# An attention and MLP kernel ordered by a list scheduler: one batch's attention cut in two, and new durations in the scheduler's table

## The chip, the cores and the metric

The kernel runs on one core of one Trainium2 chip. The metric is the device time in microseconds (us) of one execution. TensorE does the matrix products (PE; its weight loads are PEld), VectorE is DVE, ScalarE ACT, GpSimd POOL, and SyncE (SP) issues all DMAs, in order.

## The reference

Three parts run one after the other. `q`, `k`, `v` have 4 batches, 8 heads, 576 rows and 64 columns; the two MLPs see 2304 rows of width 512.

```
scores = scale * q @ k.T                        # 576 x 576 for each of 32 heads
kth    = the 32nd largest score of a row
attn   = softmax(scores where scores >= kth)
x      = (attn @ v), heads side by side         # 2304 x 512

h = x @ w_in;  x = (h * cos(h)) @ w_out         # first MLP: 512 -> 2048 -> 512

P = exp(x @ w_gate - max); 8 rounds of row and column normalisation over all 2304 rows
out = sum over 8 experts e of P[:, e] * (max(x @ w1[e], 0) @ w2[e])   # 512 -> 1024 -> 512 each
```

The column sums of `P` need the logits of all rows, so the weighted sum over experts can't be finished before the last row has left the first MLP. The products of the experts themselves need no `P`.

## The kernel before, in words

Rows are counted in tiles of 128, 18 in all. The stages, in program order:

1. Decoding: `w_in` and `w_out` come as 64-bit floats and are turned to 32 bits on DVE, ACT and POOL (`decode`, 32 blocks).
2. The first three tiles of batch 0 (`LEAD`): attention and first MLP in plain fp32 (`attention_tile`, `moe1_tile_a`, `moe1_tile_b`; L629, L638 and L654 are their matrix products).
3. `attention(0, 3)`: the other rows of batch 0. Here and below each fp32 number is split in a high and a low part, and a product is three passes (L372 to L374; L383, L384, L387).
4. `fill(e, 0, 3)` for 8 experts: the first three tiles through every expert, unweighted, kept in DRAM (`y_d`) until `P` is known. These products read `x2fh` and `x2fl`.
5. `attention(1)`, then the first MLP for rows 384 to 895 (`moe1(Part(384))`: "the second block"). Its input is read back from DRAM (`x_d`) by `load_cols` into `xh` and `xl`, 4 pieces of 128 columns; piece d holds the head pair d.
6. `attention(2)`, `attention(3)`, and `fill(e, 3, 4)` for 8 experts: the second block through the experts.
7. The other three blocks of the first MLP, the normalisation, and the experts for the other 11 tiles.

In `attention` a head pair at a time is prepared (`prep_head`: keys, queries and values are loaded and split, on ACT and POOL). A row tile then goes through `att_tile`: scores on PE (L447, L448), copied by ACT; the 32nd largest is found on DVE by MAX8 (L459, L465) and MATCH_REPLACE (L464) in turn; the mask and row sum are one DVE instruction (L466); PE transposes the weights (L475), ACT and DVE split them (L493, L494). `att_out` multiplies with the values (L501 and L503, 9 matrix products for a head and group of rows), and the result is stored to `x_d`. Rows 0 to 255 and rows 256 to 575 of a head are such groups. A tile is 128 rows of one head, or the last 64 rows of two heads.

The order on each engine is fixed at build time. Every operation is put on a list with an estimated duration, and `Plan.issue` plays the list through: whichever engine is free first takes, of the operations whose inputs are ready by the estimates, the one with the lowest number in `PRIORITY` (L29), then the earliest in the program. On PE the order is first attention, first MLP, later attention, later MLP; on DVE the MLPs come ahead of later attention. The estimates are only used for the order: at run time each engine takes its instructions one by one and waits where an input is late.

An operation's inputs are known by buffer and interval. `load_cols` depends on the stores to `x_d` that overlap its rows: rows 384 to 895 are batch 0's rows 384 to 575 and batch 1's rows 0 to 319, so that in the kernel before it waits for both row groups of a head of batch 1, the second of which ends at row 575. Its input piece d is waited for on its own, since the products of the four pieces are separate operations (L701 to L710).

Of the kernel before, what the change touches and what calls it, by code (L numbers as in the profile page):

```python
# [12 lines left out]
I32 = mybir.dt.int32  # L13
# [57 lines left out]
class Plan:  # L71
# [78 lines left out]
    def issue(self):  # L150
        ops = self.ops
        for op in ops:
            op.outs, op.left, op.ready = [], len(op.deps), 0.0
        for k, op in enumerate(ops):
            for d in op.deps:
                ops[d].outs.append(k)
        engines = ("PE", "ACT", "DVE", "POOL", "SP")
        soon = {e: [] for e in engines}
        now = {e: [] for e in engines}
        free = dict.fromkeys(engines, 0.0)  # L160
        dma_free, func, warm, window, busy = 0.0, None, False, -1, {}
        for k, op in enumerate(ops):
            if not op.left:
                heapq.heappush(soon[op.eng], (0.0, k))
        order = []
        while len(order) < len(ops):
            best = None
            for e in engines:
                if now[e]:
                    t = free[e]  # L170
                elif soon[e]:
                    t = max(free[e], soon[e][0][0])
                else:
                    continue
                if best is None or t < best[0]:
                    best = (t, e)
            t, e = best
            while soon[e] and soon[e][0][0] <= t:
                k = heapq.heappop(soon[e])[1]
                heapq.heappush(now[e], (ops[k].prio, k))  # L180
            k = heapq.heappop(now[e])[1]
            op = ops[k]
            cost = op.cost
            if op.func and op.func != func:
                cost, func = cost + 1283.0, op.func
            if e == "PE":
                w = int(t / 3413)
                if w != window:
                    past = busy.get(w - 1, 0.0) / 3413
                    warm = past > 0.95 or (warm and past > 0.5)  # L190
                    window = w
                cost *= 1.0 if warm else 2.0
                a = t
                while a < t + cost:
                    z = min(t + cost, (int(a / 3413) + 1) * 3413.0)
                    busy[int(a / 3413)] = busy.get(int(a / 3413), 0.0) + z - a
                    a = z
            free[e] = op.end = t + cost
            if e == "SP":
                dma_free = max(t + cost + 650.0, dma_free) + op.bytes / 360.0  # L200
                op.end = dma_free + 900.0
            order.append(k)
            for o in op.outs:
                n = ops[o]
                n.ready = max(n.ready, op.end + self.LAT.get((e, n.eng), 130.0))
                n.left -= 1
                if not n.left:
                    heapq.heappush(soon[n.eng], (n.ready, o))
        self.estimate = max(op.end for op in ops)
        for k in order:  # L210
            ops[k].emit()


def mm_ns(n):
    return max(107.0, n / 2.4 + 3.0)


def act_ns(n, psum=False, ap=False):
# [11 lines left out]
def fused_kernel(tc, kq, vv, w_in, w_out, w_gate, w1, w2, out, B=4):  # L230
# [84 lines left out]
    def decode(src, keep, part):  # L315

        raw, mag, sgn, low = d_raw(), d_mag(), d_sgn(), d_low()  # L320
        dma(lambda: raw.ap, lambda: src.bitcast(I32), 1 << 19, writes=[raw])
        hi = lambda dt: raw.ap.bitcast(dt).rearrange("p (n t) -> p n t", t=2)[:, :, 1]
        lo = lambda: raw.ap.bitcast(U32).rearrange("p (n t) -> p n t", t=2)[:, :, 0]
        magf = lambda: mag.ap.bitcast(F32)
        put("DVE", 335, lambda: V.tensor_scalar(mag.ap, hi(I32), 3, 0x40000000, op0=ALU.logical_shift_left, op1=ALU.bitwise_xor), [raw], [mag])
        put("ACT", 613, lambda: A_.activation(sgn.ap, hi(F32), AF.Identity, bias=cols.ap[:, 1:2]), [raw, cols], [sgn])
        put("ACT", 613, lambda: A_.activation(sgn.ap, sgn.ap, AF.Sign, bias=cols.ap[:, 2:3]), [sgn, cols], [sgn])
        put("ACT", 520, lambda: A_.activation(low.ap, lo(), AF.Copy, scale=2.0**-52), [raw], [low])
        put("ACT", 520, lambda: A_.activation(magf(), magf(), AF.Abs), [mag], [mag])
        put("POOL", 1225, lambda: G_.tensor_tensor(magf(), magf(), sgn.ap, op=ALU.mult), [mag, sgn], [mag])  # L330
        put("DVE", 335, lambda: V.tensor_scalar(sgn.ap.bitcast(I32), mag.ap, -8388608, None, op0=ALU.bitwise_and), [mag], [sgn])
        put("POOL", 1225, lambda: G_.tensor_tensor(low.ap, low.ap, sgn.ap, op=ALU.mult), [low, sgn], [low])
        put("POOL", 1225, lambda: G_.tensor_tensor(low.ap, magf(), low.ap, op=ALU.add), [mag, low], [low])
        dma(keep, lambda: low.ap, 1 << 18, [low], [part])
# [84 lines left out]
    rr_r = ring_of("m1", 3, [128, 1024], F32, "rr")  # L419
    tt_r = ring_of("m1", 1, [128, 1024], F32, "tt")  # L420

    def prep_head(b, h):
        bh = b * H + h
        raw, kh, kl, qs, qt, vraw, vs = (r() for r in (kq_r, kh_r, kl_r, qs_r, qt_r, vraw_r, vs_r))
        dma(lambda: raw.ap, lambda: kq[bh], 1024 * S, writes=[raw])
        split_cols((kh, lambda: kh.ap), (kl, lambda: kl.ap), (raw, lambda: raw.ap[:, 0, :]), S)
        for o, lo, c0, n in ((qs, 0, 0, 512), (qt, 64, 512, 64)):
            v = lambda r, o=o, lo=lo, n=n: o.ap[r, lo : lo + n]
            w = lambda r, c0=c0, n=n: raw.ap[r, 1, c0 : c0 + n]
            put("ACT", act_ns(n), lambda v=v, w=w: A_.activation(v(slice(0, 128)), w(slice(0, 128)), AF.Copy), [raw], [o])  # L430
            put("POOL", pool_ns(n), lambda v=v, w=w: G_.tensor_tensor(v(slice(64, 128)), w(slice(64, 128)), v(slice(64, 128)).bitcast(F32), op=ALU.subtract), [raw, o], [o])
        dma(lambda: vraw.ap, lambda: vv[bh], 128 * 1280, writes=[vraw])
        split_cols(((vs, 0, 1), lambda: vs.ap[:, :, 0:64]), ((vs, 1, 2), lambda: vs.ap[:, :, 64:128]), (vraw, lambda: vraw.ap), 5 * D)
        return dict(kh=kh, kl=kl, qs=qs, qt=qt, vs=vs)

    def att_tile(stats, dests, plain=None):
# [24 lines left out]
        put("ACT", act_ns(S, ap=True), lambda: A_.activation(ex.ap, sc.ap, AF.Exp, scale=0.125, bias=mc(32)), [sc, (m, 32, 33)], [ex], func="exp")  # L461
        for r in range(3):
            src = wk if r else sc
            put("DVE", 669, lambda r=r, src=src: V.match_replace(wk.ap, mc(8 * r, 8), src.ap, LOWEST), [src, (m, 8 * r, 8 * r + 8)], [wk])  # L464
            put("DVE", 669, lambda r=r: V.max(mc(8 * r + 8, 8), wk.ap), [wk], [(m, 8 * r + 8, 8 * r + 16)])  # L465
        put("DVE", 729, lambda: V.scalar_tensor_tensor(ex.ap, sc.ap, mc(31), ex.ap, op0=ALU.is_ge, op1=ALU.mult, accum_out=mc(33)),  # L466
            [sc, ex, (m, 24, 32)], [ex, (m, 33, 34)])
        put("POOL", 162, lambda: G_.tensor_scalar(mc(34), mc(33), 1e-9, 1.0, op0=ALU.add, op1=ALU.mult), [(m, 33, 34)], [(m, 34, 35)])
        put("DVE", 75, lambda: V.reciprocal(mc(35), mc(34)), [(m, 34, 35)], [(m, 35, 36)])  # L469
# [65 lines left out]
        work = "mlp"  # L535
        return x_f

    def attention(b, done=0):

        nonlocal work  # L540
        work = "attention"
        for pr in range(4):
            hds = [prep_head(b, 2 * pr + j) for j in range(2)]

            def begin(hd):
                hd["ath"], hd["atl"] = ath_r(), atl_r()

            def end(j, s0, n, pr=pr, hds=hds):
                x32 = x32_r()
                att_out(hds[j], x32, j, n)  # L550
                t0 = b * S + s0
                r = slice(64 * j, 64 * j + 64)
                dma(lambda: x_d.ap[r, pr, t0 : t0 + n], lambda: x32.ap[r, :n], 256 * n, [x32],
                    [(x_d, (2 * pr + j) * NT + t0, (2 * pr + j) * NT + t0 + n)], slow=True)

            for t0 in (0, 2):
                tiles = range(max(t0, done), t0 + 2)
                for j, hd in enumerate(hds):
                    if tiles or t0:
                        begin(hd)  # L560
                    for t in tiles:
                        att_tile([(hd["qs"], t * 128, hd)], [(0, 128, hd, (t - tiles[0]) * 128)])
                    if tiles and not t0:
                        end(j, tiles[0] * 128, 128 * len(tiles))
            n = 128 * len(tiles)
            att_tile([(hds[0]["qt"], 64, hds[0]), (hds[1]["qt"], 0, hds[1])], [(0, 64, hds[0], n), (64, 64, hds[1], n)])
            for j in range(2):
                end(j, 512 - n, 64 + n)
        work = "mlp"


# [433 lines left out]
    n0 = LEAD * 128  # L1005
    for e in range(NE):
        fill(e, 0, LEAD, two)
    attention(1)
    eng_g = "DVE"
    moe1(Part(n0, two, keep_parts(x2fh, x2fl)), 3)  # L1010
    eng_g = "POOL"
    for b in range(2, B):
        attention(b)
    for e in range(NE):
# [79 lines left out]
```

## Time and profile before

| | |
|---|---|
| median of 3 runs | 2482.4 us (2480.79 to 2483.55) |
| profiled execution | 2480.47 us |
| its span, first to last instruction | 2478.7 us |
| PE, DVE busy in the span | 2364.7 us, 1986.9 us |
| ACT, POOL busy in the span | 1271.7 us, 1266.6 us |

The profile is of one execution. Its page gives busy times and the span in 40 slices; the trace behind it can be asked for the busy time of each engine in any stretch, for what an engine waited for, and for single instructions in order of time. A matrix product on PE is drawn longer than it occupies the array: in a run of them the next one starts before the last has ended, so the distance between two starts is what one costs, and gaps of less than about 0.2 us don't show as idle time.

### The profile page before, as it was taken

How to read it: one execution, taken by the hardware profiler on the slowest of the kernel's cores; microseconds unless marked ns; L12 is line 12 of the kernel's file. 1: busy time of each engine (PE TensorE's matmuls, PEld its weight loads, DVE VectorE, ACT ScalarE, POOL GpSimd, SP SyncE). 2: the span in 40 equal slices, each digit the busy share in tenths (PEclk: the TensorE clock that was granted, in tenths of full speed). 3: DMA queues.
4: the chain of work that ended last, by engine and by line, in shares of the span. 5: the costliest groups of instructions: out<-in, count | busy, mean ns of one | idle time of the engine just before them, and what ended most of it. 6: DMA issues, size and time to landing. Idle time of an engine off the chain costs nothing.

```text
span 2478.7 us, 33516 instructions
## 1 busy us (share of the span) xinstructions
PE 2364.7 (95%) x11089; PEld 1905.7 (77%) x11089; DVE 1986.9 (80%) x3651; ACT 1271.7 (51%) x2438; POOL 1266.6 (51%) x1328
## 2 busy tenths in 40 slices
PE   6878999999889999999999999999999999999999
PEld 3434688888667877778878888788888888888887
DVE  8997599999998999999986787776666666666655
ACT  6785566666578666666566776322322222322221
POOL 6886487767577656656520033433443334443330
PEclk9889999999899999999999999999999999999999
DMA  8765654444323333333334333022222221111101
GB/s 263 232 210 186 200 167 144 139 123 151 109 74 97 114 115 115 115 119 97 97 114 123 91 108 104 27 64 81 81 85 81 73 60 35 36 42 43 35 22 47
DMA packets 159501, 261.37 MB, mean 105 GB/s; under 512 B 15008, under 2 KB 60656, under 8 KB 159328
## 3 DMA queue, kind: packets, MB, share of 16 engines
q1 hardware_dynamic: 159328, 259.24, 34.5%
q8 instruction: 87, 1.43, 0.2%
q14 instruction: 86, 0.70, 0.1%
HBM read 227.31 MB, written 31.87 MB: 105 GB/s over the span
## 4 chain that ended last, share of the span: by engine, by line
PE 57%; DVE 28%; POOL 6%; issue 4%; ACT 3%; DMA 1%; SPq 0%; POOLq 0%; ACTq 0%; DVEq 0%
PE y L372 9%; PE y L373 9%; PE y L374 9%; DVE wk L464 7%; DVE m L465 6%; DVE ex L466 4%; PE g L374 2%; PE g L373 2%; PE g L372 2%; DVE m L459 2%; POOL wlo L347 2%; DVE atl L494 1%; PE y L383 1%; PE y L387 1%; PE y L384 1%
## 5 line engine op out<-in xcount | busy, mean ns | idle before, releaser
L347 POOL TENSOR_TENSOR wlo<-raw,whi 128x512 fp32r<-128x512 f32 x336 | 451.7, 1349 | 195.1 <-ACT whi L345 116.3
L465 DVE MAX8 m<-wk 128x8 f32<-128x576 f32 x432 | 318.1, 748 | 1.9
L953 DVE SCALAR_TENSOR_TENSOR acc<-y,P,acc 128x512 f32<-128x512 f32 x308 | 229.2, 748 | 103.5 <-PE y L374 103.2
L345 ACT ACTIVATE whi<-raw 128x512 fp32r<-128x512 f32 x416 | 259.2, 627 | 96.5 <-PE y L374 36.9
L464 DVE MATCH_REPLACE8 wk<-m,wk 128x576 f32<-128x576 f32 x288 | 213.5, 742 | 1.1
L372 PE MATMUL y<-whi,gh 128*128 128x512 f32 x448 | 182.0, 406 | 0.0
L372 PE MATMUL y<-gh,xh 128*128 128x512 f32 x450 | 177.1, 393 | 1.0 <-DVE acc L949 1.0
L374 PE MATMUL y<-whi,gl 128*128 128x512 f32 x448 | 176.5, 394 | 0.0
L373 PE MATMUL y<-gl,xh 128*128 128x512 f32 x450 | 176.5, 392 | 0.0
L374 PE MATMUL y<-gh,xl 128*128 128x512 f32 x450 | 176.2, 392 | 0.0
L373 PE MATMUL y<-wlo,gh 128*128 128x512 f32 x448 | 176.0, 393 | 0.0
L475 PE MATMUL t<-ident,ex 128*128 128x128 f32 (+1 forms) x720 | 136.6, 290 | 39.7 <-POOL ex L470 10.9
L457 ACT ACTIVATE sc<-s 128x288 f32<-128x288 f32 x288 | 117.0, 406 | 95.6 <-DVE ex L466 54.9
L475 PEld LDWEIGHTS t<-ident,ex 128*128 128x128 f32 (+1 forms) x720 | 85.9, 140 | 101.6 <-POOL ex L470 27.8
L466 DVE SCALAR_TENSOR_TENSOR ex<-sc,m,ex 128x576 f32<-128x576 f32 x144 | 152.8, 1061 | 3.6 <-ACT ex L461 1.8
L470 POOL TENSOR_SCALAR ex<-ex,m 128x576 f32<-128x576 f32 x144 | 111.2, 772 | 33.9 <-DVE m L469 33.0
L493 ACT ACTIVATE ath<-t 64x128 fp32r<-64x128 f32 (+3 forms) x272 | 104.5, 396 | 46.2 <-PE t L475 40.0
L461 ACT ACTIVATE ex<-sc,m 128x576 f32<-128x576 f32 x144 | 111.3, 773 | 32.4 <-POOL m L460 31.4
L459 DVE MAX8 m<-sc 128x8 f32<-128x576 f32 x144 | 106.9, 743 | 9.2 <-ACT sc L457 9.1
L464 DVE MATCH_REPLACE8 wk<-m,sc 128x576 f32<-128x576 f32 x144 | 106.7, 741 | 0.0
L372 PEld LDWEIGHTS y<-gh,xh 128*128 128x128 f32 x450 | 85.2, 189 | 20.0 <-DVE acc L949 1.8
L372 PE MATMUL y<-gh,gh 128*128 128x512 f32 x254 | 99.4, 391 | 0.0
(376 smaller groups left out, 7054.6 us busy)
## 6 DMA issues: line engine op xcount, KB each, us to landing
raw<-in_w_dram SPq DMA_DIRECT2D x384, 256.0 KB, 2.6
kq<-in_kq_dram SPq DMA_DIRECT2D x32, 576.0 KB, 4.3
raw<-win_d SPq DMA_DIRECT2D x64, 256.0 KB, 3.0
raw<-wout_d SPq DMA_DIRECT2D x64, 256.0 KB, 2.7
y_d<-st SPq DMA_DIRECT2D x56, 256.0 KB, 3.0
raw<-y_d SPq DMA_DIRECT2D x56, 256.0 KB, 2.7
wp<-win_d SPq DMA_DIRECT2D x24, 512.0 KB, 5.3
wp<-wout_d SPq DMA_DIRECT2D x24, 512.0 KB, 4.4
```

The costliest lines, as they stand in the source:

```text
L345: put("ACT", act_ns(n), lambda: A_.activation(hv(), rv(), AF.Copy), [rb], [hb])
L347: put(e, c, lambda: f.tensor_tensor(lv(), rv(), hv().bitcast(F32), op=ALU.subtract), [rb, hb], [lb])
L372: T_.matmul(o(), ah(), bh(), start=start, stop=False)
L373: T_.matmul(o(), ah(), bl(), start=False, stop=False)
L374: T_.matmul(o(), al(), bh(), start=False, stop=stop)
L457: put("ACT", act_ns(288, psum=True), lambda c=c: A_.activation(sc.ap[:, c], o(), AF.Copy), [ps_s], [(sc, c.start, c.stop)])
L459: put("DVE", 669, lambda: V.max(mc(0, 8), sc.ap), [sc], [(m, 0, 8)])
L464: put("DVE", 669, lambda r=r, src=src: V.match_replace(wk.ap, mc(8 * r, 8), src.ap, LOWEST), [src, (m, 8 * r, 8 * r + 8)], [wk])
L465: put("DVE", 669, lambda r=r: V.max(mc(8 * r + 8, 8), wk.ap), [wk], [(m, 8 * r + 8, 8 * r + 16)])
L466: put("DVE", 729, lambda: V.scalar_tensor_tensor(ex.ap, sc.ap, mc(31), ex.ap, op0=ALU.is_ge, op1=ALU.mult, accum_out=mc(33)), [sc, ex, (m, ...
L475: T_.transpose(pt()[:p, c - c0, :], ex.ap[:, c * 128 : c * 128 + p], ident.ap)
L953: put("DVE", 663, lambda y=y, av=av, pcol=pcol: V.scalar_tensor_tensor(av(), y.ap, pcol(), av(), op0=ALU.mult, op1=ALU.add), [y, P, a], [a])
```

## The change

`attention(b, done, stop)` now takes an end as well as a start, in tiles. Batch 1 is done as `attention(1, 0, 3)`, rows 0 to 383 of each head, and `attention(1, 3)`, rows 384 to 575. Between the two calls stands the second block's first MLP, which needs rows 0 to 319 of that batch. Heads are prepared anew by each call: keys and values whole, queries only those that the call uses (also in `attention(0, 3)`). The row groups of a head of batch 1 were 256 and 320; they are 256, 128 and 192.

The durations that `Plan.issue` works with are changed in five places: the decoding's two DVE operations (335 to 600 ns, twice), a matrix product (n/2.4 + 3 to n/2.4 + 13.6 ns for n columns), MATCH_REPLACE (669 to 738), the mask with its row sum (729 to 960), and the DMA rate (360 to 280 bytes per ns). They change no instruction, only the order.

```diff
-                dma_free = max(t + cost + 650.0, dma_free) + op.bytes / 360.0
+                dma_free = max(t + cost + 650.0, dma_free) + op.bytes / 280.0
...
-    return max(107.0, n / 2.4 + 3.0)
+    return max(107.0, n / 2.4 + 13.6)
...
-    def prep_head(b, h):
+    def prep_head(b, h, q0, q1):
...
-        for o, lo, c0, n in ((qs, 0, 0, 512), (qt, 64, 512, 64)):
+        for o, lo, c0, n in [(qs, q0, q0, min(q1, 512) - q0)] + [(qt, 64, 512, 64)] * (q1 > 512):
...
-    def attention(b, done=0):
+    def attention(b, done=0, stop=5):
...
-            hds = [prep_head(b, 2 * pr + j) for j in range(2)]
+            hds = [prep_head(b, 2 * pr + j, done * 128, min(stop * 128, S)) for j in range(2)]
...
-                tiles = range(max(t0, done), t0 + 2)
+                tiles = range(max(t0, done), min(t0 + 2, stop))
+                last = t0 and stop == 5
...
-                    if tiles or t0:
+                    if tiles or last:
...
-                    if tiles and not t0:
+                    if tiles and not last:
                         end(j, tiles[0] * 128, 128 * len(tiles))
-            n = 128 * len(tiles)
-            att_tile([(hds[0]["qt"], 64, hds[0]), (hds[1]["qt"], 0, hds[1])], [(0, 64, hds[0], n), (64, 64, hds[1], n)])
-            for j in range(2):
-                end(j, 512 - n, 64 + n)
+            if stop == 5:
+                n = 128 * len(tiles)
+                att_tile([(hds[0]["qt"], 64, hds[0]), (hds[1]["qt"], 0, hds[1])], [(0, 64, hds[0], n), (64, 64, hds[1], n)])
+                for j in range(2):
+                    end(j, 512 - n, 64 + n)
...
-    attention(1)
+    attention(1, 0, 3)
     eng_g = "DVE"
     moe1(Part(n0, two, keep_parts(x2fh, x2fl)), 3)
     eng_g = "POOL"
+    attention(1, 3)
```

Three places show what becomes of the order. The numbers behind a name are those of a buffer.

PE at the start of the second block's first MLP, in the kernel before: `g` and `h` are the banks of its first two products over `xh`, `ath` and `atl` with 320 columns are batch 1's last head pair, `t<-ident,ex` are transposes of tiles of batch 2.

```order
L374 MATMUL g<-xh,wlo_1715 128x512
L372 MATMUL h<-xh,whi_1691 128x512
...
L374 MATMUL h<-xh,wlo_1726 128x512
L447 MATMUL s<-kh_1400,qs_1405 128x288
...
L501 MATMUL t<-ath_1604,vs_1393 128x320
...
L501 MATMUL t<-ath_1722,vs_1416 128x320
...
L475 MATMUL t<-ident,ex_189 128x128 x4
...
L372 MATMUL g<-xh,whi_1687 128x512
L373 MATMUL g<-xl,whi_1687 128x512
```

The same place in the kernel after the change:

```order
L374 MATMUL g<-xh,wlo_1809 128x512
L475 MATMUL t<-ident,ex_185 128x128 x4
L372 MATMUL g<-xh,whi_1779 128x512
L373 MATMUL g<-xl,whi_1779 128x512
L374 MATMUL g<-xh,wlo_1809 128x512
L447 MATMUL s<-kh_1265,qs_1269 128x288
L448 MATMUL s<-kl_1299,qs_1269 128x288
L372 MATMUL g<-xh,whi_1779 128x512
L373 MATMUL g<-xl,whi_1779 128x512
L374 MATMUL g<-xh,wlo_1809 128x512
L372 MATMUL h<-xh,whi_1783 128x512
```

Before, the first two products stop after three of their four pieces, and 39 rows of attention work stand ahead of the fourth piece. After, all four pieces follow each other, with single steps of attention between them.

SP at the same place, in the kernel before: `raw<-x_d` are the four pieces of the second block's input, `x_d<-x` the stores of attention results.

```order
L266 DMA raw_146<-x_d 128x512
L266 DMA x_d<-x_1973 64x256
...
L266 DMA raw_132<-x_d 128x512
L266 DMA raw_146<-win_d 128x4x128
...
L266 DMA x_d<-x_1933 64x320
L266 DMA vraw_120<-in_v_dram 128x320
L266 DMA x_d<-x_1973 64x320
L266 DMA vraw_125<-in_v_dram 128x320
L266 DMA raw_139<-x_d 128x512
L266 DMA raw_139<-win_d 128x4x128
```

And after the change:

```order
L266 DMA x_d<-x_1895 64x192
...
L266 DMA raw_143<-x_d 128x512
L266 DMA raw_146<-x_d 128x512
L266 DMA raw_132<-x_d 128x512
L266 DMA raw_143<-win_d 128x4x128
L266 DMA raw_134<-x_d 128x512
L266 DMA raw_146<-win_d 128x4x128
L266 DMA raw_141<-win_d 128x4x128
L266 DMA raw_132<-win_d 128x4x128
L266 DMA x_d<-x_1853 64x192
```

The fourth piece stood behind the two stores of batch 1's last head pair. Now all four stand ahead of the last such pair (the stores of 192 columns), which are rows that the block doesn't read.

PE near the end of the plain first MLP, before the change: `y_1232<-wp,gT_1242` are the second tile's second products (L654, L656 after the change), `rr` the third tile's gated values, which are transposed for its own second products.

```order
L629 MATMUL y_353<-wp_512,x_f_277 128x512 x2
L654 MATMUL y_1232<-wp_322,gT_1242 128x512 x2
L638 MATMUL y_766<-ident,rr_907 128x128 x4
...
L638 MATMUL y_766<-ident,rr_1152 128x128 x4
...
L654 MATMUL y_1232<-wp_512,gT_1242 128x512 x2
L475 MATMUL t<-ident,ex_137 128x128 x4
L447 MATMUL s<-kh_1400,qs_1405 128x288
L448 MATMUL s<-kl_1425,qs_1405 128x288
L661 MATMUL y_766<-ident,st_1449 128x128 x4
```

And after it:

```order
L631 MATMUL y_400<-wp_497,x_f_260 128x512 x2
L475 MATMUL t<-ident,ex_139 128x128 x4
L447 MATMUL s<-kh_1248,qs_1255 128x288
...
L656 MATMUL y_1219<-wp_330,gT_1236 128x512 x2
L640 MATMUL y_805<-ident,rr_866 128x128 x4
...
L475 MATMUL t<-ident,ex_139 64x128
...
L447 MATMUL s<-kh_1265,qs_1269 128x288
...
L475 MATMUL t<-ident,ex_185 128x128 x4
```

Steps of `attention(0, 3)` that stood behind the second tile's 16 second products now stand ahead of them and among them. Up to the first product of the first `fill`, PE has 28 score products of later attention, where it had 12, and 134 transposes, where it had 125.

## Rows read from the trace of the kernel before

**Rows 1.** The page's first part: busy us, share and instructions of two engines.
```profile
PE 2364.7 (95%) x11089; PEld 1905.7 (77%) x11089; DVE 1986.9 (80%) x3651; ACT 1271.7 (51%) x2438; POOL 1266.6 (51%) x1328
```

**Rows 2.** Busy us by stage: length, engines, then PE clock, DMA share, GB/s.
```profile
225.00:285.00 60.00, 55.26 (x191) 27.62 (x190) 21.84 (x40) 23.22 (x41) 16.12 (x22) 0.97 0.60 194
293.00:650.00 357.00, 349.68 (x1966) 309.74 (x1967) 347.96 (x774) 244.46 (x537) 279.81 (x323) 1.00 0.49 147
653.00:683.00 30.00, 18.56 (x68) 14.27 (x67) 29.32 (x69) 14.07 (x34) 11.06 (x21) 0.66 0.15 44
683.00:815.00 132.00, 116.64 (x555) 91.74 (x554) 120.54 (x203) 101.47 (x170) 96.31 (x88) 0.99 0.29 84
815.00:1275.00 460.00, 454.00 (x2277) 367.77 (x2276) 448.61 (x973) 280.57 (x594) 274.34 (x345) 1.00 0.38 114
1275.00:1450.00 175.00, 172.91 (x760) 140.41 (x760) 127.47 (x183) 117.66 (x181) 16.93 (x12) 1.00 0.35 105
1450.00:1600.00 150.00, 139.36 (x701) 122.77 (x699) 114.97 (x209) 84.57 (x151) 60.11 (x46) 0.97 0.26 77
1600.00:2450.00 850.00, 849.02 (x3862) 715.96 (x3861) 542.65 (x771) 232.05 (x405) 328.82 (x284) 1.00 0.18 54
```

**Rows 3.** PE in order of time, 652 to 679 us: start, duration, idle before.
```profile
652.85 0.39 PE L372 MATMUL h<-xh,whi 128*128 128x512 f32 x1
...
656.33 0.40 PE L447 MATMUL s<-kh,qs 128*128 128x288 f32 x1 [2.64 <-ACT sc L457]
...
673.42 0.42 PE L475 MATMUL t<-ident,ex 128*64 128x128 f32 x1 [2.38 <-DVE atl L494]
...
678.01 0.63 PE L372 MATMUL g<-xh,whi 128*128 128x512 f32 x1
678.44 0.63 PE L373 MATMUL g<-xl,whi 128*128 128x512 f32 x1
```

**Rows 4.** SP's own waits, 640 to 700 us: total, times, longest us.
```profile
SPq L266 <- DVE x L509: 15.1, 2, 12.3
```

**Rows 5.** SP in order of time, 671 us.
```profile
671.89 0.33 SPq L266 DMA_DIRECT2D raw<-x_d  x1
```

**Rows 6.** Busy us by stage, as in rows 2: five us inside the gap.
```profile
660.00:665.00 5.00, 4.38 (x14) 3.41 (x14) 4.93 (x14) 1.69 (x5) 0.94 (x2) 0.50 0.00 0
```

**Rows 7.** PE's waits, 700 to 820 us: total, times, longest us.
```profile
PE t L475 <- DVE atl L494: 6.7, 6, 2.2
PE t L475 <- DVE ath L494: 2.8, 2, 1.7
PE t L475 <- DVE x L509: 1.7, 1, 1.7
```

**Rows 8.** PE in order of time: value products of 192, 320 and 256 columns.
```profile
307.49 0.28 PE L503 MATMUL t<-atl,vs 128*128 128x192 f32 x1
...
308.27 0.28 PE L501 MATMUL t<-ath,vs 128*128 128x192 f32 x1
...
592.51 0.30 PE L501 MATMUL t<-ath,vs 128*128 128x320 f32 x1
...
593.68 0.31 PE L501 MATMUL t<-ath,vs 128*128 128x320 f32 x1
...
610.26 0.28 PE L501 MATMUL t<-ath,vs 128*128 128x256 f32 x1
...
611.21 0.28 PE L501 MATMUL t<-ath,vs 128*128 128x256 f32 x1
```

**Rows 9.** POOL's groups by form, head preparation: count, busy us, mean ns, idle before.
```profile
L347 POOL TENSOR_TENSOR kl<-kq,kh 128x576 fp32r<-128x576 f32 x32 | 47.8, 1494 | 7.2 <-DMA wp<-win_d 3.4 <-ACT kh L345 2.8
L431 POOL TENSOR_TENSOR qs<-kq,qs 64x512 fp32r<-64x512 f32 x32 | 42.9, 1342 | 21.7 <-ACT qs L430 17.6 <-POOL m L468 0.7 <-POOL m L460 0.6
L347 POOL TENSOR_TENSOR vs<-vraw,vs 128x320 fp32r<-128x320 f32 x32 | 31.5, 986 | 12.1 <-ACT vs L345 11.2
L431 POOL TENSOR_TENSOR qt<-kq,qt 64x64 fp32r<-64x64 f32 x32 | 12.4, 386 | 2.5
```

**Rows 10.** Busy us, as in rows 2: the start of `attention(0, 3)`.
```profile
300.00:325.00 25.00, 24.17 (x141) 21.33 (x140) 23.45 (x53) 18.86 (x46) 23.78 (x26) 1.00 0.51 142
```

**Rows 11.** DVE's L466 alone, busy us (two records a tile), by stage.
```profile
229.00:285.00 56.00, 1.65 (x4) 0.97 0.62 202
293.00:650.00 357.00, 47.35 (x90) 1.00 0.49 147
```

**Rows 12.** DMA issues: count, KB each, median us to landing.
```profile
kq<-in_kq_dram SPq DMA_DIRECT2D x32, 576.0 KB, 4.3
vraw<-in_v_dram SPq DMA_DIRECT2D x32, 160.0 KB, 2.4
```

More of the change, by code (lines that the diff above doesn't have):

```diff
@@ L324, in decode @@
         magf = lambda: mag.ap.bitcast(F32)
-        put("DVE", 335, lambda: V.tensor_scalar(mag.ap, hi(I32), 3, 0x40000000, op0=ALU.logical_shift_left, op1=ALU.bitwise_xor), [raw], [mag])
+        put("DVE", 600, lambda: V.tensor_scalar(mag.ap, hi(I32), 3, 0x40000000, op0=ALU.logical_shift_left, op1=ALU.bitwise_xor), [raw], [mag])
         put("ACT", 613, lambda: A_.activation(sgn.ap, hi(F32), AF.Identity, bias=cols.ap[:, 1:2]), [raw, cols], [sgn])
@@ L330, in decode @@
         put("POOL", 1225, lambda: G_.tensor_tensor(magf(), magf(), sgn.ap, op=ALU.mult), [mag, sgn], [mag])
-        put("DVE", 335, lambda: V.tensor_scalar(sgn.ap.bitcast(I32), mag.ap, -8388608, None, op0=ALU.bitwise_and), [mag], [sgn])
+        put("DVE", 600, lambda: V.tensor_scalar(sgn.ap.bitcast(I32), mag.ap, -8388608, None, op0=ALU.bitwise_and), [mag], [sgn])
         put("POOL", 1225, lambda: G_.tensor_tensor(low.ap, low.ap, sgn.ap, op=ALU.mult), [low, sgn], [low])
@@ L463, in att_tile @@
             src = wk if r else sc
-            put("DVE", 669, lambda r=r, src=src: V.match_replace(wk.ap, mc(8 * r, 8), src.ap, LOWEST), [src, (m, 8 * r, 8 * r + 8)], [wk])
+            put("DVE", 738, lambda r=r, src=src: V.match_replace(wk.ap, mc(8 * r, 8), src.ap, LOWEST), [src, (m, 8 * r, 8 * r + 8)], [wk])
             put("DVE", 669, lambda r=r: V.max(mc(8 * r + 8, 8), wk.ap), [wk], [(m, 8 * r + 8, 8 * r + 16)])
-        put("DVE", 729, lambda: V.scalar_tensor_tensor(ex.ap, sc.ap, mc(31), ex.ap, op0=ALU.is_ge, op1=ALU.mult, accum_out=mc(33)),
+        put("DVE", 960, lambda: V.scalar_tensor_tensor(ex.ap, sc.ap, mc(31), ex.ap, op0=ALU.is_ge, op1=ALU.mult, accum_out=mc(33)),
             [sc, ex, (m, 24, 32)], [ex, (m, 33, 34)])
```

## The prediction

> **What bounds the kernel now.** I read the page's busy shares first, then the busy time by stage, then the waits and single instructions of the one stage that stood out. PE is busy 2364.7 of 2478.7 us [rows 1], so some 114 us at most are to be had by keeping it fed. By stage [rows 2] the reader is to see three things. From 293 to 650 us, and again from 815 to 1275, PE and DVE are both above 97%: attention runs on DVE, and the experts' products fill PE between the steps of attention. From 1275 to 1450 us DVE has dropped to 127.5 of 175 us while PE stays at 172.9: attention is over and the experts' products still aren't, so PE alone sets the end from there, and from 1600 on it has no gap at all. Hence each microsecond of PE time that is lost before 1275 us, and isn't DVE's to give, arrives at the end in full. The third thing is the hole between: from 653 to 683 us PE is busy 18.56 of 30 us, at a mean clock of 0.66, with DVE at 29.3.
>
> The single instructions of the hole [rows 3] show its cause. The second block's first products run until 653 us, three of the four pieces of each; the fourth piece's product starts at 678.01. Between them PE has only attention, whose pace is DVE's. SP waits 15.1 us for the additions at L509, once for 12.3 us [rows 4], then loads the missing piece at 671.89 [rows 5]. So the block waited for the last head pair of batch 1, through DVE, a store and a load; and since the load depends on both row groups of the head, it waited for rows that it doesn't read.
>
> **The change, part by part.** Times are against the profiled execution, 2480.5 us; the median of the runs shown is 1.9 us above it.
>
> *The hole closes.* In the new order the four pieces are loaded ahead of the stores of rows 384 to 575, and depend only on rows that were finished some 12 tiles earlier. In the hole PE idles 30 - 18.56 = 11.4 us [rows 2]. The rest is attention that has to be done anyway, but slowly: the clock has two levels, in the five us from 660 on it is at the lower, 1.2 GHz (0.50) [rows 6], and a 512-column product takes 678.44 - 678.01 = 0.43 us [rows 3], where 512 columns at 2.4 GHz are 0.21. A mean of 0.66 is 0.68 of the stretch at the lower level. Half of what ran at that level is lost: between 0.68 x 18.56 / 2 = 6.3 and, if all work fell there, 9.3; I take 8, since the first seven us, at the higher level, hold little work. Term: -19.4 us. What is late next is the gated values: the block's second products can't start before its first have gone through the gate.
>
> *Inside the second block* PE idles another 132 - 116.64 = 15.4 us [rows 2], 11.2 of them in transposes that wait for DVE [rows 7]. There the planned order runs ahead of DVE. The new table makes a tile longer on DVE (three MATCH_REPLACE at +69 ns and a mask at +231 are 0.44 us) and PE's products about 5% longer, so the balance between the two hardly moves. Bounds 0 and -11.2; nearest to the row that the same stage shows, little changes: -3.
>
> *More value products.* A head of batch 1 now has three row groups for two: nine more products, 72 for eight heads, the columns being the same. From the starts [rows 8]: 320 columns cost (593.68 - 592.51) / 8 = 0.146 us, 256 cost (611.21 - 610.26) / 8 = 0.119, 192 cost (308.27 - 307.49) / 7 = 0.111. No row shows 128. From below, in proportion to columns, it is 0.059; from above the cost of 192, 0.111, to which the step from 256 to 192 points (64 columns fewer save 0.008). With 0.111 a head gains 9 x (0.111 + 0.111 - 0.146) = 0.68 us, eight heads 5.5; with 0.059, 1.7. I take +5.5: it falls where PE is 98% busy, with nothing to hide behind. The Trainium skill (TensorE: Matmul & The Clock Gate, Back-to-back issue gap) has about 81 ns for a sustained product of 128 columns with its weight load, which makes an estimate of 3.3 us for this term; no run here shows 128 columns yet, and the sum keeps the row.
>
> *Heads prepared twice.* Batch 1 adds 8 key and 8 value splits on POOL; with the queries cut to what is used, 16 splits of 512 columns become 8 of 384 and 16 of 128. From 1342 ns for 512 and 386 for 64 columns [rows 9] these are 1069 and 523 ns. Sum: 8 x 1494 + 8 x 986 - 16 x 1342 + 8 x 1069 + 16 x 523 = 15.3 us more POOL work. What hides it is POOL's idle time, 357 - 279.8 = 77 us in that stage [rows 2]; it comes bunched, though, with 12 tiles of work among eight preparations. The same mix ran at the start of `attention(0, 3)`: POOL 23.8 of 25 us, PE idle 0.83 [rows 10]. At 347.96 / 45 = 7.7 us of DVE per tile (45 tiles by the count of masks) [rows 2, 11], 12 tiles last 93 us, and 0.83 of 25 over them is 3 us; `attention(0, 3)` itself gets lighter. Bounds 0 and +15.3, taken +2. The copies on ACT (244 of 357 us) have more room than POOL. The reloads, 8 x 736 KB [rows 12], meet DMA engines that are half idle. DVE's eight more additions make attention end later, which the 175 us after it cover.
>
> *The first MLP's end.* Steps of `attention(0, 3)`, 16 score products and 9 transposes, move ahead of the first `fill`. In 225 to 285 us PE idles 4.7 us and DVE 38.2 [rows 2], so the work finds room; what PE does there it needn't do later. Bounds: -4.7, and on the other side the third rival. Taken -2.
>
> *The rest of the order* shifts by the new table with no side that I can name. Idle PE time in the four other stages of rows 2 from 293 to 1600 us is 7.3 + 6.0 + 2.1 + 10.6 = 26 us; a fifth of it either way, 5 us, bounds it. Taken 0.
>
> Sum: -19.4 - 3 + 5.5 + 2 - 2 = -16.9; 2480.5 - 16.9 = 2463.6, and with 1.9 to the median 2465.5: I say 2465.
>
> **Rivals.**
>
> *The hole moves into the gate.* The block starts on time, but its second products wait: a pair of first products goes through POOL, DVE, ACT, DVE, ACT and DVE again, and DVE has attention queued between. For it: inside the block PE already idles 15.4 us, with DVE at 120.5 of 132. Against it: as many first products (66 for 63) stand ahead of the first second product as before, and some attention. If half the hole comes back, 2465.5 + 10 = 2475.
>
> *DVE sets the pace.* If the two attention stages were DVE's, a fuller PE would end the experts' work no earlier. For it: DVE 97% in both. Against it: the 175 us in which PE works on alone. The gain would be nothing, the extra products mostly hidden: 2482.
>
> *PE stuck in the first MLP (slower).* PE takes its queue in order. Two tiles' transposes now stand among the second tile's second products, ahead of all of the third tile's, and another one's before the end of those. If PE arrives before a tile has left DVE, the whole first MLP stands still, and with it the first `fill`. Price at worst: three tiles in sequence at 7.7 us, 23 us, so 2465.5 + 23 = 2488; it outweighs the gain from 17 us of such waiting on. For it: PE's waits inside the second block are of this kind [rows 7]. Against it: DVE is idle most of this stage, so a tile there runs through without a queue.
>
> **How the numbers follow.** The forecast has 0.66, its own range 2453 to 2476 (from the terms' bounds, not all at one end); the gate 0.17; DVE's pace 0.08; the stuck PE 0.09. A measurement of this kernel can tell about 0.2%, 5 us, from no change: faster is below 2477.4, slower above 2487.4. Faster: 0.97 x 0.66 + 0.85 x 0.17 + 0.1 x 0.08 = 0.79, rounded to 0.80; slower 0.09, since a part of the stuck case is milder and a part of DVE's case worse; the rest, 0.11, is the same. The range ends at 2481, which leaves out the stuck PE and half of DVE's case, and begins at 2449, where the hole closes, the second block's waits go and the value products cost their lower bound: 2482.4 - 19.4 - 11.2 + 1.7 - 4.7 = 2448.8.
>
> **What would show it.** Right: from the first products over `xh` on no idle stretch of PE over a few us, all four pieces loaded before the last `fill` of the first round ends, PE's clock at 1.0 through 645 to 685 us, the second block over some 15 to 20 us earlier (815 us now), and the last experts' stage as long as before. The value products' starts give the price of 128 columns, the stretch before 285 us whether PE waits there at transposes. Wrong: a first `fill` that starts later than 290 us, POOL full with PE waiting at `wlo` where rows 384 to 575 are worked on, or new waits for the gate at L383.

## The result and the profile after

The changed kernel takes 2497.75 us (median of 4 runs, 2495.57 to 2500.96), the kernel before 2482.39 beside it: ratio 1.0063, interval 1.0046 to 1.0081. It is slower by 15 us, where 17 us less were forecast. The profiled execution has a span of 2495.6 us against 2478.7, so the two traces show +16.9 us between them.

The page's first line after, to be held against [rows 1]: PE has 72 products more, as counted, and 19.3 us more busy time.

```profile
PE 2384.0 (96%) x11161; PEld 1910.2 (77%) x11161; DVE 2024.2 (81%) x3659; ACT 1281.2 (51%) x2470; POOL 1279.6 (51%) x1352
```

The busy time by stage after, cut at this kernel's own borders (first `fill` product 304.8 us, second block 684.6 to 811.8), to be held against [rows 2].

```profile
225.00:305.00 80.00, 73.45 (x279) 38.35 (x278) 57.86 (x119) 35.83 (x74) 23.83 (x39) 0.96 0.57 187
305.00:684.00 379.00, 366.55 (x2083) 319.66 (x2083) 363.08 (x800) 259.78 (x586) 301.15 (x350) 1.00 0.53 157
684.00:812.00 128.00, 112.95 (x534) 88.51 (x533) 120.71 (x209) 100.12 (x167) 101.28 (x91) 0.99 0.31 92
812.00:1275.00 463.00, 457.49 (x2285) 367.62 (x2285) 454.35 (x973) 282.02 (x594) 277.77 (x348) 1.00 0.38 110
1275.00:1450.00 175.00, 168.66 (x745) 136.45 (x744) 124.73 (x187) 113.64 (x180) 14.07 (x12) 1.00 0.35 103
1450.00:1600.00 150.00, 140.79 (x708) 125.01 (x707) 116.91 (x193) 92.39 (x163) 58.16 (x43) 0.97 0.31 90
1600.00:2450.00 850.00, 846.46 (x3853) 713.35 (x3853) 567.57 (x794) 234.63 (x409) 326.48 (x289) 1.00 0.19 54
```

The hole of [rows 3] is gone. The loads of the four pieces are issued by 671 us, 14 us ahead of the block, and PE stands full at the higher clock where the block begins (SP in order of time, then a stretch of the stages).

```profile
662.48 5.14 SPq L266 DMA_DIRECT2D raw<-x_d  x3
670.69 0.32 SPq L266 DMA_DIRECT2D raw<-x_d  x1
```

```profile
645.00:685.00 40.00, 39.95 (x228) 35.03 (x227) 37.67 (x90) 28.52 (x65) 32.62 (x37) 1.00 0.54 155
```

The loss is earlier. From 75 to 200 us PE is busy equally long in both kernels, but at a mean clock of 0.67 for 0.84, and gets 282 products done for 350; DVE is busy 9 us less. The first row is the kernel before.

```profile
75.00:200.00 125.00, 101.23 (x350) 49.88 (x349) 121.33 (x222) 99.97 (x186) 106.54 (x107) 0.84 0.72 220
```

```profile
75.00:200.00 125.00, 101.30 (x282) 49.23 (x281) 111.97 (x193) 87.08 (x160) 103.58 (x101) 0.67 0.62 190
```

By line over the same 125 us, before and then after (count, busy us, mean ns, idle before): a first-attention tile has ten products at L530, so 14 tiles are done before and 11 after, and the first MLP's 512-column products get longer. DVE waits more often for POOL's part of the decoding (L331).

```profile
L530 PE MATMUL t<-at_f,vp 128*64 128x128 f32 (+1 forms) x140 | 22.8, 306 | 4.7 <-ACT at_f L479 4.7
L629 PE MATMUL y<-wp,x_f 128*128 128x512 f32 x28 | 18.4, 748 | 1.8 <-ACT x_f L534 1.8
L331 DVE TENSOR_SCALAR d_sgn<-d_mag 128x512 int32<-128x512 int32 x21 | 16.9, 803 | 1.6 <-POOL d_mag L330 1.6
```

```profile
L530 PE MATMUL t<-at_f,vp 128*64 128x128 f32 (+1 forms) x110 | 24.2, 381 | 1.8 <-ACT at_f L479 1.8
L631 PE MATMUL y<-wp,x_f 128*128 128x512 f32 x25 | 19.6, 883 | 1.4 <-ACT x_f L534 1.4
L331 DVE TENSOR_SCALAR d_sgn<-d_mag 128x512 int32<-128x512 int32 x20 | 21.3, 1071 | 5.5 <-POOL d_mag L330 5.5
```

Five instants tell where time goes in any of these kernels. All are starts read from groups of one tile: the first and last `fill` product over `x2fh` (L372), the second block's first product over `xh`, its end (the gating product `g<-x2fh,wg`), and the last attention mask (L466). Before against after: first fill 285.2 and 304.8 (+19.6); from there to the block 364.0 and 379.8 (+15.8); the block 151.3 and 127.2 (-24.1); from it to the last fill product 462.3 both; the last mask 4.2 and 7.9 us behind that (+3.7); all the rest +1.9. Sum +16.9.

### The profile page after: what moved, and what is told of

The parts are those of the page before. It is cut to its first block, busy times and chain, and to the rows that moved or that the text cites. A ratio compares the mean times of both kernels' runs of the same rounds, so it can differ in the third digit from the quotient of the medians.

```text
span 2495.6 us, 33757 instructions
## 1 busy us (share of the span) xinstructions
PE 2384.0 (96%) x11161; PEld 1910.2 (77%) x11161; DVE 2024.2 (81%) x3659; ACT 1281.2 (51%) x2470; POOL 1279.6 (51%) x1352
## 4 chain that ended last, share of the span: by engine, by line
PE 52%; DVE 5%; ACT 2%; POOL 1%; issue 1%; DMA 0%; POOLq 0%; ACTq 0%; DVEq 0%
PE y L372 8%; PE y L374 8%; PE y L373 8%; PE g L374 2%; PE g L373 2%; PE g L372 2%; PE y L383 1%; PE y L384 1%; PE y L387 1%; PE y L888 1%; PE s L887 1%; PE y L887 1%; PE h L889 1%; PE h L887 1%; PE y L889 1%; PE s L889 1%
## 5 line engine op out<-in xcount | busy, mean ns | idle before, releaser
L347 POOL TENSOR_TENSOR wlo<-raw,whi 128x512 fp32r<-128x512 f32 x336 | 457.9, 1366 | 225.5 <-ACT whi L345 138.2
L345 ACT ACTIVATE whi<-raw 128x512 fp32r<-128x512 f32 x416 | 259.6, 627 | 101.3 <-PE y L374 34.5
L372 PE MATMUL y<-whi,gh 128*128 128x512 f32 x448 | 183.0, 409 | 0.7 <-ACT gh L760 0.7
L372 PE MATMUL y<-gh,xh 128*128 128x512 f32 x450 | 176.5, 392 | 0.3 <-DVE acc L951 0.3
L475 PE MATMUL t<-ident,ex 128*128 128x128 f32 (+1 forms) x720 | 138.1, 292 | 33.6 <-POOL ex L470 15.4
L466 DVE SCALAR_TENSOR_TENSOR ex<-sc,m,ex 128x576 f32<-128x576 f32 x144 | 163.7, 1137 | 1.6
L372 PEld LDWEIGHTS y<-gh,xh 128*128 128x128 f32 x450 | 84.9, 189 | 19.2 <-DVE acc L951 1.1
L372 PE MATMUL y<-gh,gh 128*128 128x512 f32 x254 | 99.3, 391 | 0.0
```

Source lines behind the costliest of these rows:

```text
L345: put("ACT", act_ns(n), lambda: A_.activation(hv(), rv(), AF.Copy), [rb], [hb])
L347: put(e, c, lambda: f.tensor_tensor(lv(), rv(), hv().bitcast(F32), op=ALU.subtract), [rb, hb], [lb])
L372: T_.matmul(o(), ah(), bh(), start=start, stop=False)
L466: put("DVE", 960, lambda: V.scalar_tensor_tensor(ex.ap, sc.ap, mc(31), ex.ap, op0=ALU.is_ge, op1=ALU.mult, accum_out=mc(33)), [sc, ex, (m, ...
L475: T_.transpose(pt()[:p, c - c0, :], ex.ap[:, c * 128 : c * 128 + p], ident.ap)
```

## The experiments

The change has two halves, the split of batch 1's attention and five numbers of the scheduler's table. Theory T1 lays the loss on the table, T2 on the split's own work. Letters stand for the entries: B the transfers' rate (360 to 280 bytes a ns), M a product (+10.6 ns), D the two decoding operations on DVE (335 to 600), R match_replace (669 to 738), S the mask (729 to 960). Profiled instants in us:

| kernel | median us | ratio to before, interval | first fill | block from, to | last fill | last mask |
|---|---|---|---|---|---|---|
| before | 2481.2 | | 285 | 649, 800 | 1263 | 1267 |
| after (BMDRS) | 2497.75 | 1.0063, 1.0046 to 1.0081 | 305 | 685, 812 | 1274 | 1282 |
| split_only | 2470.0 | 0.9954, 0.9940 to 0.9969 | 290 | 671, 798 | 1254 | 1260 |
| table_only | 2496.0 | 1.0061, 1.0046 to 1.0076 | 302 | 673, 811 | 1275 | 1272 |
| split_justB | 2477.6 | 0.9989, 0.9980 to 0.9999 | 296 | 675, 798 | 1261 | 1261 |
| split_justM | 2515.9 | 1.0139, 1.0124 to 1.0154 | 286 | 684, 822 | 1294 | 1242 |
| split_justD | 2490.3 | 1.0035, 1.0022 to 1.0047 | 285 | 661, 787 | 1257 | 1278 |
| split_justR | 2506.3 | 1.0107, 1.0091 to 1.0124 | 285 | 657, 780 | 1242 | 1305 |
| split_justS | 2489.8 | 1.0035, 1.0022 to 1.0049 | 286 | 654, 787 | 1246 | 1288 |
| split_BD | 2470.5 | 0.9959, 0.9944 to 0.9974 | 286 | 662, 787 | 1251 | 1259 |
| split_MR | 2497.2 | 1.0061, 1.0044 to 1.0078 | 279 | 665, 799 | 1274 | 1260 |
| split_MS | 2497.1 | 1.0062, 1.0047 to 1.0077 | 280 | 662, 797 | 1273 | 1264 |
| split_noD (BMRS) | 2504.3 | 1.0094, 1.0079 to 1.0109 | 285 | 665, 791 | 1260 | 1301 |
| split_noB (MDRS) | 2524.2 | 1.0172, 1.0157 to 1.0188 | 294 | 675, 804 | 1270 | 1315 |
| early_new | 2491.2 | 1.0045, 1.0029 to 1.0062 | 293 | 671, 803 | 1266 | 1284 |
| late_new | 2483.7 | 1.0008, 0.9998 to 1.0017 | 284 | 667, 799 | 1264 | 1270 |
| eMR_m5 | 2478.65 | 0.9991, 0.9982 to 1.0000 | 282 | 661, 792 | 1264 | 1270 |
| eMR_m6 | 2481.1 | 1.0001, 0.9992 to 1.0010 | 279 | 662, 791 | 1263 | 1262 |

The median of before is that over 25 runs beside the experiments.

**Each half alone, and the decoding's entry.** In split_only the five numbers go back; table_only has the new numbers and the attention in one part; split_noD and split_justD move D alone. The edit of split_only to the kernel after (table_only is its reverse on the kernel before):

```diff
-                dma_free = max(t + cost + 650.0, dma_free) + op.bytes / 280.0
+                dma_free = max(t + cost + 650.0, dma_free) + op.bytes / 360.0
-    return max(107.0, n / 2.4 + 13.6)
+    return max(107.0, n / 2.4 + 3.0)
-        put("DVE", 600, lambda: V.tensor_scalar(mag.ap, ...
+        put("DVE", 335, lambda: V.tensor_scalar(mag.ap, ...
...
-            put("DVE", 738, lambda r=r, src=src: V.match_replace(...
+            put("DVE", 669, lambda r=r, src=src: V.match_replace(...
-        put("DVE", 960, lambda: V.scalar_tensor_tensor(ex.ap, ...
+        put("DVE", 729, lambda: V.scalar_tensor_tensor(ex.ap, ...
```

> The attention of the second batch is split as in the kernel after, but the five old durations stand in the scheduler's table. Theory T1 (the table's new numbers reorder the first 305 us and that is the loss): the first fill product comes at about 285 us again, the second block starts at about 655 and ends at about 785, and the time is about 2465 us, 17 below before. Theory T2 (the split's own extra work, heads prepared twice and shorter value products, lengthens the fill stage by its 15 us): the fill stage stays near 379 us, the second block's gain of 24 us is mostly eaten, and the time is about 2477 to 2485 us.

> The attention of the second batch stays in one part; only the five durations in the scheduler's table are the new ones. T1: first fill product at about 305 us as in the kernel after, the hole at the start of the second block stays, and the time is about 2500 to 2515 us, slower than after. T2: the first fill product is late only by what the second block's tiles pulled forward cost, and the time is within 5 us of before, 2478 to 2488 us.

> The kernel after with one entry put back: the two decoding operations of DVE count 335 again and not 600. Theory D (this entry alone moves decoding ahead of first-attention tiles): 22 tiles instead of 18 stand ahead of the first qt copy of the new decode order, the first fill product comes at about 285 to 290 us, and the time is 2465 to 2475 us. Theory B or M (another entry does it): first fill product at about 300 us or later, time 2488 to 2500 us.

> The split with the old table, but the two decoding operations of DVE count 600. Theory D: first fill product at 300 us or later and a time of 2485 to 2500 us. If another entry does it: first fill product at about 285 us, time about 2465 us, as the split with the old table is to have under T1.

The split alone gains 11.2 us, the table alone loses 14.8: T1 holds for where the loss comes from. Its times don't: split_only was to take 2465 and table_only 2500 to 2515 us. On the new table the split is worth nothing that can be told (2496.0 and 2497.75). That D alone makes the first fill late falls, since D alone has it at 285; but all but D has it at 285 too, so the 305 of the kernel after needs D together with other entries. Both kernels still lose, at the end of the attention. A part of T2 holds: split_only's fill stage (first fill to the second block) is as long as after's, 381.1 us for 379.8, though its block is shorter than before's by 24.4.

**One entry at a time.** The split with the old table and one new number, as

```diff
-    return max(107.0, n / 2.4 + 3.0)
+    return max(107.0, n / 2.4 + 13.6)
```

for M, and likewise for the others.

> The split with the old table, but the scheduler counts transfers at 280 bytes a ns and not 360. Theory one-entry (a single second entry, this one, is what costs beside the decoding's): 2480 us or more. Theory sensitive order (the order of before was fitted to its own table, and any entry that moves instructions near a handover between stages loses there): between 2470 and 2495 us, with the loss at one of four places, the first fill product (290 us with the old table), the second block's first product (671), its end (798) or the last fill product (1254), and a different place than for the other entries.

> The split with the old table, but each product of TensorE counts 10.6 ns more. Every product moves alike, so theory one-entry has no reason for a loss here: 2468 to 2474 us. Theory sensitive order: 2470 to 2495 us, lost at one of the four handovers.

> The split with the old table, but match_replace counts 738 and not 669; 207 ns more for each attention tile on DVE. Theory one-entry: 2468 to 2476 us. Theory sensitive order: 2470 to 2495 us, and since a tile counts more, attention tiles lag and the last of them ends later against the last fill product (1260 and 1254 us with the old table).

> The split with the old table, but the masking operation of each attention tile counts 960 and not 729; 231 ns more for each tile on DVE, about as much as the change of match_replace. Both theories expect about the same time as for match_replace alone, within 6 us, if what counts is the sum on DVE for each tile; a larger difference speaks for an order that answers to anything.

Over split_only the single entries cost 8 (B), 46 (M), 20 (D), 36 (R) and 20 us (S), 130 together; all five at once cost 28. So they don't add, and theory one-entry falls with M, which had no reason to cost anything. Theory sensitive order is nearer, but M and R lie above its 2470 to 2495 us as well. R and S add nearly the same to a tile on DVE and lie 16.5 us apart, not within 6. What the runs share is where they lose: a heavier DVE entry lets the attention lag behind the fill, a heavier product the reverse. The two groups in the two extreme runs, split_justR and then split_justM (durations, then the first and the last start):

```profile
L372 PE MATMUL g<-x2fh,whi x256: 332/392/669, 284.9 to 1241.9; 128*128 128x384 f32 x64, 128*128 128x512 f32 x64
L466 DVE SCALAR_TENSOR_TENSOR ex<-sc,m,ex x144: 794/820/1966, 19.2 to 1305.2; 128x576 f32<-128x576 f32 x144
```

```profile
L372 PE MATMUL g<-x2fh,whi x256: 332/393/481, 286.3 to 1294.0; 128*128 128x384 f32 x64, 128*128 128x512 f32 x64
L466 DVE SCALAR_TENSOR_TENSOR ex<-sc,m,ex x144: 790/941/1941, 17.0 to 1241.7; 128x576 f32<-128x576 f32 x144
```

In split_justR the fills are done 63 us before the attention, and PE then has nothing to put between its steps (a stage row, then two of its longest waits in order of time): 31 of 88 us idle, and a clock of 0.79.

```profile
1262.00:1350.00 88.00, 56.71 (x234) 43.83 (x233) 63.20 (x119) 41.58 (x68) 5.22 (x13) 0.79 0.16 45
```

```profile
1297.03 1.11 PE L475 MATMUL t<-ident,ex 128*128 128x128 f32 x4 [10.55 <-POOL ex L470]
...
1303.77 1.11 PE L475 MATMUL t<-ident,ex 128*128 128x128 f32 x4 [3.80 <-POOL ex L470]
```

In split_justM it is DVE that has run out, busy 19.7 of 70 us, while PE still has fills to do:

```profile
1240.00:1310.00 70.00, 70.00 (x316) 57.42 (x315) 19.72 (x35) 31.03 (x59) 26.70 (x23) 1.00 0.46 141
```

**Pairs.** The edits are those above, two at a time (four for split_noB).

> The split with the old table, but with two entries new: transfers at 280 bytes a ns and decoding operations at 600. Theory pair (these two together make the late first fill, since neither does alone: 296 us and 285 us): first fill product at 300 us or later, and since the last attention products stand close behind the last fill product in TensorE's order (4 groups of them), the stages end together and the time is 2485 to 2500 us. Rival (the late first fill needs the three other entries): first fill at 285 to 297 us and a time of 2470 to 2482 us.

> The kernel after with the transfers counted at 360 bytes a ns again. Theory pair: first fill product at 284 to 291 us, 14 to 20 us earlier than in the kernel after; but 10 groups of attention products stand behind the last fill product in TensorE's order (4 in the kernel after), so the attention ends some 35 to 45 us behind the last fill product (at about 1295 to 1300 us), and the time is 2495 to 2510 us in spite of the early fill. Rival (transfers' entry matters nowhere but in the first stage): the 14 to 20 us are gained at the end, 2478 to 2484 us.

> The split with the old table, but with two entries new that cost 46 and 36 us when each stood alone: TensorE's products and match_replace. Theory balance (alone the first lets the attention end 52 us ahead of the last fill product and the second 63 us behind it, and the time follows the later of the two): together both end within 15 us of each other, the later at 1255 to 1272 us, and the time is 2465 to 2482 us. Rival (each entry costs by itself): the losses add, 2535 to 2555 us.

> The same with the masking operation in place of match_replace; alone it costs 20 us, with the attention 42 us behind the last fill product. In TensorE's order the last attention products now stand 18 rows before the last fill product. Theory balance: both end within 12 us of each other, the later at 1255 to 1270 us, time 2465 to 2480 us. Rival (each entry costs by itself): 2525 to 2545 us.

B and D together have the early first fill (286), so theory pair falls; they also cost nothing, where D alone cost 20. split_noB was mildly late at the first fill (294) and its attention ended 45 us behind the fill, as TensorE's order had said; the time was worse than either theory. M with R or with S: both ends lie within 14 us of each other, as theory balance has it, and M's 46 and R's 36 become 27. But the time is above the 2465 to 2482 expected, since with M the stage from the block to the last fill product takes 475 us for 456, and the rest behind it 1219 to 1222 for 1208. So balance is one part only. In all 18 profiles the later of the table's last two columns runs from 1259 to 1315 us, and what follows it only from 1199 to 1222: most of the difference is settled by the time both are done.

**Which stage's numbers, and a table put together.** A switch chooses the table while the program is written out: early_new has the five new numbers up to the first `qt` copies and the old ones behind, late_new the reverse; eMR_m5 and eMR_m6 have M and R before that point and a product at +2 or +3 ns behind it.

```diff
+def entry(k):
+    return TABLE[k][k in TABLE["now"]]
...
+    TABLE["now"] = "BMDRS"
...
+    TABLE["now"] = ""
     for qt in qt_r.bufs:
```

> The split; the scheduler counts with the five new durations for all work up to the first qt copies (decoding, first attention, first MLP) and with the old ones for all that is written after them. Theory early (the first stage's own durations make it late): first fill product at 298 to 305 us. Theory late (the work after it, pulled in ahead of the first fill, does): 280 to 292 us. By TensorE's order 6 groups of attention products stand behind the last fill product, where the kernel with the old table has 4 and those with 7 to 10 lost 20 to 45 us: so the time is about 2480 to 2490 us by the second theory and 2490 to 2505 by the first.

> The reverse: old durations up to the first qt copies, the five new ones after them. Theory early: first fill product at 284 to 292 us as with the old table, 4 attention groups behind the last fill product, and a time of 2470 to 2482 us. Theory late: first fill product at 298 to 305 us and a time of 2488 to 2500 us.

> The split; up to the first qt copies the old table with the two entries of products and match_replace new (they had the first fill product at 279 us, 11 earlier than the old table), and after them the old table with a product at 2 ns more, which leaves 4 groups of attention products behind the last fill product in TensorE's order, as with the old table. Theory two separate losses (a late first fill, and attention and fill ending apart): first fill at about 279 us, attention's end within 15 us of the last fill product, and a time of 2455 to 2466 us, under both kernels and the split with the old table. Rival (an early first fill is given back in the fill stage, which DVE and TensorE pace together): 2467 to 2478 us.

> The same with a product at 3 ns more after the first stage; 2 groups of attention products stand behind the last fill product. Theory two separate losses: first fill at about 279 us, and a time within 8 us of the run with 2 ns more, 2455 to 2470 us. Rival (the order answers to anything, and the place of the last groups says little of the time): further apart than 8 us.

New early numbers alone make the first fill 293, new late ones 284, both 305: the late first fill is not the sum of the two. Theory late falls with the 284, and the 293 falls short of the 298 to 305 of theory early. Why both are needed stays open. The two built tables had the early first fill, and gave it back: from the block to the last fill product they take 472 us for split_only's 456. So two separate losses falls; the rival comes nearest (2478.65 against its 2467 to 2478), and eMR_m6 lies 2.4 us off eMR_m5, inside its 8. The version that beats both kernels remains the split with the old table, 11.2 us under before (split_BD is level with it).

## Why the prediction was wrong, by its steps

- **The first MLP's end, taken -2, was +19.6.** This is the step that failed: 21.6 of the 33.8 us between the forecast and the two traces. It looked at the room in 225 to 285 us and at what moves into it, and left the other side to the rival of the stuck PE. It did not ask what the new table does before that: by 200 us three first-attention tiles fewer are done, 16 of 24 for 19, and PE works at the lower of its two levels for longer. The table does it, not the split (302 us with the table alone, 290 with the split alone); the decoding's new price is needed for it, but isn't enough (285 without it, and 285 with it alone). How the entries act together stays open. The rival of the stuck PE had the side (2488), but not the mechanism. From 75 us to the first fill (before, then after) PE isn't idle longer, 31.3 us for 33.5; it is busy 21.7 us longer.

```profile
75.00:285.20 210.20, 176.75 (x624) 88.00 (x622) 167.61 (x306) 139.18 (x255) 142.64 (x147) 0.89 0.67 211
```

```profile
75.00:304.80 229.80, 198.48 (x656) 99.53 (x654) 189.79 (x354) 143.68 (x271) 141.50 (x159) 0.81 0.61 191
```

From the clocks of 75 to 200 us, 101.2 x 0.84 = 85 us of full-speed work stand against 101.3 x 0.67 = 68: an estimate of 17 us, near the 19.6. But the same working gives 14 us for split_justD (100.3 x 0.71) and 23 for split_noB (98.5 x 0.63), whose first fills start 0.3 us earlier and 8.6 later than before's. So it isn't shown that the clock is the cause. The tiles go along with the first fill more closely: 16 by 200 us in the kernel after and in table_only (305 and 302), 17 in split_noB and early_new (294 and 293), 18 or more in the other 14 (279 to 290, but 296 in split_justB).
- **The rest of the order, taken 0 with a fifth of the idle time as bound,** was the same mistake in another place: the idle time of before doesn't bound what another order does. Behind the block the two traces differ by +5.6 us, just past the bound. The runs measure the whole: with the split unchanged and only numbers of the table moved, the time goes from 2470 to 2524 us.
- **The hole closes and the second block: -22.4 forecast, -24.1 measured.** The cause was right, and table_only shows that it isn't only the split's: there the block still shrinks by 12.9 us. It starts 24 us later, with 73 tiles masked for 71, though its fourth piece is still loaded only after its start (at 678 us, the start being 673). The waits inside the block stayed: 128 - 112.95 = 15.05 us idle for 15.4.
- **What it costs before the block was mis-sized: 5.5 + 2 forecast, +15.8 measured.** The fill stage masks 45 tiles in both kernels, yet it is longer, and both engines that fill it are (before, then after):

```profile
285.20:649.20 364.00, 355.37 (x2000) 314.33 (x1998) 352.90 (x785) 249.25 (x551) 286.57 (x331) 1.00 0.49 147
```

```profile
304.80:684.60 379.80, 367.35 (x2088) 320.34 (x2086) 363.69 (x801) 260.58 (x587) 301.95 (x350) 1.00 0.53 157
```

PE is busy 12.0 us more and idle 3.8 more. Of the 12.0 an estimate of 8 us is value products, 288 for 198 at the prices of [rows 8]: besides the new row groups, those of the last head pair, which ran in the hole before, now stand here. So that part of the hole's work was not gained but moved. DVE is busy 10.8 us more, 5.4 of it in the same 45 masks, which take longer. The rival that DVE sets the pace may have part of the truth; which of the two engines sets it here isn't shown. The split is the larger part: the stage takes 381.1 us in split_only and 371.0 in table_only. From the first fill to the block's end PE is busy 479.5 of 507.0 us, 480.5 of 515.3 before: the gain is 8.3 us where 14.9 were forecast. split_only, without the table, has 7.3 here, 7.6 more behind the block, and 4.6 against it at the first fill.
- **More value products, +5.5: right in its price.** 128 columns cost (466.65 - 465.98) / 6 = 0.111 us, the upper bound, the same as 192 in [rows 8]. The Trainium skill's 81 ns (TensorE: Matmul & The Clock Gate, Back-to-back issue gap) is not what these products show.

```profile
465.98 0.27 PE L501 MATMUL t<-ath,vs 128*128 128x128 f32 x1
...
466.65 0.28 PE L501 MATMUL t<-ath,vs 128*128 128x128 f32 x1
```

- **Heads prepared twice, +2:** the sizes were right, 1087 and 500 ns for 1069 and 523. POOL's busy time in the fill stage rises by 15.4 us for the 15.3 of the sum, and POOL still has 78 of 379 us free there. What PE lost to it can't be told from the rest: its idle time in the stage goes from 8.6 to 12.5 us. POOL's groups after, 312 to 684 us:

```profile
L431 POOL TENSOR_TENSOR qs<-kq,qs 64x384 fp32r<-64x384 f32 x8 | 8.7, 1087 | 0.6
...
L431 POOL TENSOR_TENSOR qs<-kq,qs 64x128 fp32r<-64x128 f32 x10 | 5.0, 500 | 0.8
```

Of what the prediction said to look for, the signs for the hole came: no long idle stretch of PE in the block, four pieces early, the clock at 1.0. The second block was not over 15 to 20 us earlier, though, but 11 us later (811.8 for 800.5), and the sign against it came too, a first `fill` later than 290 us.

## What to carry to other kernels

A number in a scheduler's table is not a cost but a choice of order: here the new numbers cost more than the edit beside them gains (28 us on the split's 11), and the profile of before didn't show the side. Change the table and the program apart and time each, and give a term like "the rest of the order" the spread that a few such tables show, not a share of the idle time. And price where the work from a closed hole goes: here the block became 24 us shorter and the stage ahead of it, with two engines near 96%, 16 us longer.

## What the runs showed of the hardware

- The mask of the same shape (L466, 128 x 576) takes from 789 to over 2000 ns, its median over a run from 820 to 972 ns, with the same instructions in another order (split_justR and late_new); the 45 masks of the fill stage have a mean of 1165 ns after, 1044 before. So a table of durations depends on the order that it makes. The Trainium skill (GPSIMD Engine Reference, Specifications) says that POOL and VectorE share their memory interfaces and that DVE's operations with two such inputs contend; the mask is one of these, but no run here varies POOL's work by itself. The masks of the fill stage, before and then after:

```profile
L466 DVE SCALAR_TENSOR_TENSOR ex<-sc,m,ex 128x576 f32<-128x576 f32 x45 | 47.0, 1044 | 0.5
```

```profile
L466 DVE SCALAR_TENSOR_TENSOR ex<-sc,m,ex 128x576 f32<-128x576 f32 x45 | 52.4, 1165 | 0.6
```

- A product of 128 columns costs as much as one of 192, 0.111 us, each with its own weights.
